# Attention scores, transposes and features in pairs of PSUM banks, emptied by one wide instruction each, and a new order of the work

## The chip, the cores and the metric

One core of a Trainium2 chip runs the whole kernel. The metric is the device time of one execution in microseconds (us). The engines are TensorE (PE; its weight loads are PEld), VectorE (DVE), ScalarE (ACT), GpSimd (POOL) and SyncE (SP, which here only issues DMAs).

## What is computed

Attention over 4 batches and 8 heads (768 positions, head size 64) with a mask from hashed buckets, followed by a gated MLP:

```
q_bucket, k_bucket = sign bits of q @ proj, k @ proj (6 bits)
scores = where(q_bucket == k_bucket, q @ k.T / 8, -1e9)
attn   = softmax(scores) (sum + 1e-9);  o = attn @ v;  x = heads of o side by side
h = gelu(x @ w_in);  u, v = halves of h;  v_n = layernorm(v) * g_ln
out = x + (u * (w_sg @ v_n + b_sg)) @ w_out
```

## The kernel before, in words

**Stages.** The attention works on 16 pairs of heads. For a pair, `parts` transposes q and k on PE (L475), and splits each into a high part (ACT, L479) and a low part (DVE, L482). `features` turns them into bucket features (PE L497, DVE L500). `largest` makes, for each of 6 tiles of 128 queries, scores with the queries on the partitions (PE L517) and takes the negative maximum of each row (DVE L524). `shift` joins the maxima of three tiles (DVE L532, L533), spreads them over columns (PE L539) and writes them into a row of the query features (ACT L545). `weigh` makes the scores again with the keys on the partitions (PE L560), now shifted by that row; ACT takes their exponentials (L566), and POOL adds these up (L576). `weighted` multiplies them with v (PE L589); `finish` sums over partitions (PE L604), copies sums and products out (ACT L607, L609), sends the sums through DRAM, adds 1e-9 (DVE L614), inverts (L615), and scales (DVE L625, POOL L626). A half pair is 384 queries: three tiles of `largest`, six key tiles of `weigh`, one `weighted`, one `finish`.

Beside this DVE splits the MLP's input weights into high and low parts, in 16 jobs of eight DVE instructions (`weight_job`, L356 to L365, with a square on POOL, L358). Then the MLP runs batch by batch: `hidden_v` (PE L761), `hidden_u` (L793), `gate` (L811), `project` (L837, L842), each with its evacuations. `gate_weights` transposes `w_sg` once (PE L720, ACT L726, DVE L729), and `out_weights` runs 16 smaller weight jobs, after the attention's buffers are given back.

**PSUM.** There are 8 banks of 128x512 floats. Every PE group takes single banks (`ps_tile`). The two heads of a pair run side by side on the two halves of PE's rows, so a group of `largest` takes two banks (four matmuls, two a bank) and a group of `weigh` two (eight matmuls). Each bank is emptied by an instruction of its own.

**The order.** All work is added to a planner (`Plan`) in groups with a cost, a priority and dependencies; its list scheduler picks for each engine the ready group of smallest priority and writes one fixed order per engine, in which the engine then issues. Priorities come from numbers at the top of the file (L22 to L30): `AHEAD` says how many tiles `largest` runs ahead of `weigh`, `WSTEP` and `WP` when the weight jobs are due, `wg` and `wo` when gate and output weights are. An instruction whose operand isn't ready holds up what stands behind it on its engine.

```
plan.add(PE, 0.346, prio + 0.01 * kh, lambda kh=kh: mm(kh), [...], sc[kh], form="row")
for j in range(2):
    plan.add(DVE, 0.55, prio, lambda j=j, kh=kh: nc.vector.tensor_reduce(
        mx()[:, kh, i, j:j + 1], sc[kh][j]()[:, :SH], axis=AX.X, op=ALU.max, negate=True), ...)
```

Of the kernel before, what the change touches and what calls it, by code (L numbers as in the profile page):

```python
# [29 lines left out]
ADDS = ["POOL", "POOL", "POOL", "POOL", "POOL"]  # L30


class Plan:
# [68 lines left out]
    def order(self):  # L102
# [32 lines left out]
        while len(out) < len(G):  # L135
# [59 lines left out]
            for b in wants[n]:  # L195
                b.i = min(b.slots, key=b.slots.get)
                b.slots[b.i] = 1e9
            for b in g["slots"]:
                left[b] -= 1
                till[b] = max(till.get(b, 0), end)  # L200
                if not left[b]:
                    b.slots[b.i] = till[b] + self.WAIT
# [20 lines left out]
def kernel(  # L223
# [54 lines left out]
    nc.vector.memset(less, -1.0)  # L278

# [137 lines left out]
    if True:  # L417
# [18 lines left out]
        NPT = 17  # L436
        ptiles = [late.pool.tile([P, SH + 1], F32, tag=f"p{i}", name=f"p{i}", bufs=1) for i in range(NPT)]
        for i, t in enumerate(ptiles):
            (nc.vector if i % 2 else nc.gpsimd).memset(t[:, SH:SH + 1], 1.0)
# [26 lines left out]
        def parts(st, s, prio):  # L466

            hh, lo, raw, fac = st.hi[s], st.lo[s], st.raw[s], (SCALE, 1.0)[s]
            for hf in range(2):
                tp = ps_tile()  # L470
                cs = slice(hf * SH, (hf + 1) * SH)

                def tr(tp=tp, hf=hf):
                    for i in range(HT):
                        nc.tensor.transpose(tp()[:, i * P:(i + 1) * P],  # L475
                                            raw()[:, hf * HT + i].rearrange("p j d -> p (j d)"), ident)

                def high(tp=tp, cs=cs):
                    nc.scalar.mul(hh()[:, cs], tp()[:, :SH], fac)  # L479

                def low(tp=tp, cs=cs):
                    nc.vector.scalar_tensor_tensor(lo()[:, cs], tp()[:, :SH], fac, hh()[:, cs].bitcast(F32),  # L482
                                                   op0=ALU.mult, op1=ALU.subtract)

                plan.add(PE, 0.327, prio, tr, [raw, (hh, hf), (lo, hf)], [tp])
                plan.add(ACT, 0.49, prio, high, [tp], [(hh, hf)])
                plan.add(DVE, 0.55, prio, low, [tp, (hh, hf)], [(lo, hf)])

        def features(st, s, prio):
            hh, lo, ft = st.hi[s], st.lo[s], st.ft[s]  # L490
            for hf in range(2):
                cs = slice(hf * SH, (hf + 1) * SH)
                fp = ps_tile()

                def project(fp=fp, cs=cs):
                    for i, (w, x) in enumerate(((pwh, hh), (pwl, hh), (pwh, lo))):
                        nc.tensor.matmul(fp()[:, :SH], w[:, s, :], x()[:, cs], start=(i == 0), stop=(i == 2))  # L497

                def sign(fp=fp, cs=cs):
                    nc.vector.tensor_scalar(ft()[:, cs], fp()[:, :SH], fcol[:, 2 * s:2 * s + 1],  # L500
                                            fcol[:, 2 * s + 1:2 * s + 2], op0=ALU.is_gt, op1=ALU.mult)

                plan.add(PE, 0.522, prio, project, [(hh, hf), (lo, hf), (ft, hf)], [fp])
                plan.add(DVE, 0.67, prio, sign, [fp], [(ft, hf)])

        def largest(st, t, prio):
# [5 lines left out]
            sc = [[ps_tile() for j in range(2)] for kh in range(2)]  # L512

            def mm(kh):
                for n, x in enumerate((st.ft, st.hi)):
                    for j in range(2):
                        nc.tensor.matmul(sc[kh][j]()[:, :SH], x[0]()[row(j), qs], x[1]()[row(j), kh * SH:(kh + 1) * SH],  # L517
                                         start=(n == 0), stop=(n == 1))

            for kh in range(2):  # L520
                plan.add(PE, 0.346, prio + 0.01 * kh, lambda kh=kh: mm(kh),
                         [(st.hi[0], hf), (st.hi[1], kh), (st.ft[0], hf), (st.ft[1], kh)], sc[kh], form="row")
                for j in range(2):
# [381 lines left out]
```

## Time and profile before

| | |
|---|---|
| median of 3 runs | 813.07 us (812.31 to 813.81) |
| the profiled execution | 810.48 us |
| its span, first to last instruction | 808.6 us |
| PE busy | 777.6 us, 96% |
| DVE busy | 594.6 us, 74% |
| POOL busy | 446.9 us, 55% |
| ACT busy | 410.9 us, 51% |
| mean granted TensorE clock | 0.976 of full speed |

The profiled execution lies 2.6 us below the median of the runs, and its span 1.9 us below its own time. A busy time counts an instruction from its start to its end, waits inside it included. PE's busy share says little here: a matmul that waits behind another counts as busy. The granted clock is 1 at 2.4 GHz and 0.5 at 1.2 GHz.

### The profile page before, as it was taken

To read this page: it belongs to the slowest core of one execution; us is meant where nothing else is said; L and a number is where in the kernel's file an instruction comes from. 1 tells how busy PE (TensorE), PEld (TensorE's weight loads), DVE (VectorE), ACT (ScalarE), POOL (GpSimd) and SP (SyncE) were. 2 spreads that over 40 slices of the span, in tenths; PEclk is the share of its full clock that TensorE was granted. 3 is DMA by queue.
4 is the path that set the end of the run, shared out by engine and by line. 5 is a ranking of instruction groups with operands and counts; after the bars stand their busy time and mean duration, and the time that the engine had idled before them with its cause. 6 is when DMAs were issued, how large, how long until landed. Compare 5 with 4: busy or idle time off the path is not lost.

```text
span 808.6 us, 15333 instructions
## 1 busy us (share of the span) xinstructions
PE 777.6 (96%) x5480; PEld 627.0 (78%) x5480; DVE 594.6 (74%) x1241; ACT 410.9 (51%) x926; POOL 446.9 (55%) x471
## 2 busy tenths in 40 slices
PE   6999999999899999999999999699899999999998
PEld 4877776767676767777676769598898889988996
DVE  7889988797988988988998449878981268407730
ACT  2457666665465656756575655614442246214411
POOL 1459787888688868888887962332232202501130
PEclk9799999999799999999999999699999999999999
DMA  6131432243243133243311112510034220040003
GB/s 156 40 82 38 130 99 73 82 112 89 64 112 96 51 93 89 58 99 93 88 46 54 29 41 62 198 51 27 26 92 157 84 73 21 19 131 27 1 1 130
DMA packets 99307, 60.93 MB, mean 75 GB/s; under 512 B 64288, under 2 KB 91040, under 8 KB 99232
## 3 DMA queue, kind: packets, MB, share of 16 engines
q1 hardware_dynamic: 97920, 56.94, 25.6%
q10 hardware_dynamic: 1312, 3.02, 1.1%
q8 instruction: 43, 0.70, 0.4%
q14 instruction: 32, 0.26, 0.1%
HBM read 47.16 MB, written 12.78 MB: 74 GB/s over the span
## 4 chain that ended last, share of the span: by engine, by line
PE 79%; DVE 17%; DMA 1%; issue 1%; ACT 1%; ACTq 0%; SPq 0%; DVEq 0%
PE g L560 16%; PE g L589 13%; PE g L811 12%; PE g L837 8%; PE g L517 7%; PE g L761 6%; PE g L793 5%; PE g L497 4%; DVE mx L524 3%; PE g L475 3%; PE g L604 2%; PE g L539 1%; PE g L842 1%; DVE h L746 1%; DVE wx L363 1%
## 5 line engine op out<-in xcount | busy, mean ns | idle before, releaser
L576 POOL TENSOR_TENSOR sum<-sum,p 128x384 f32<-128x384 f32 x256 | 257.4, 1041 | 41.0 <-ACT p L566 40.8
L524 DVE TENSOR_REDUCE mx<-g 128x1 f32<-128x384 f32 x384 | 186.9, 549 | 27.6 <-PE g L517 22.7
L566 ACT ACTIVATE p<-g 128x384 f32<-128x384 f32 x384 | 161.4, 495 | 53.5 <-PE g L560 49.5
L589 PE MATMUL g<-p,v 128*64 128x385 f32 x768 | 131.2, 491 | 0.0
L589 PEld LDWEIGHTS g<-p,v 128*64 128x64 f32 x768 | 52.3, 137 | 64.5 <-issue 61.4
L560 PE MATMUL g<-hq,hk 64*128 64x384 f32 x384 | 81.6, 372 | 8.3 <-DVE mx L524 8.1
L517 PE MATMUL g<-fk,fq 64*128 64x384 f32 x384 | 76.4, 350 | 1.7 <-DVE mx L524 0.8
L822 POOL TENSOR_TENSOR gs<-gt,gs 128x384 fp32r<-128x384 f32 x32 | 32.9, 1031 | 76.2 <-ACT gs L819 76.2
L576 POOL TENSOR_TENSOR sum<-p,p 128x384 f32<-128x384 f32 x64 | 67.0, 1065 | 14.3 <-ACT p L566 14.3
L560 PE MATMUL g<-hq,lk 64*128 64x384 f32 x384 | 74.6, 343 | 0.0
L517 PE MATMUL g<-hk,hq 64*128 64x384 f32 x384 | 73.8, 342 | 0.0
L560 PE MATMUL g<-fq,fk 64*128 64x384 f32 x384 | 73.5, 340 | 0.0
L560 PE MATMUL g<-lq,hk 64*128 64x384 f32 x384 | 73.4, 340 | 0.0
L771 POOL TENSOR_TENSOR mv<-mv,epsr 128x1 f32<-128x1 f32 x24 | 13.5, 562 | 108.0 <-DVE mv L770 101.7
L746 DVE SCALAR_TENSOR_TENSOR h<-h,g 128x384 f32<-128x384 f32 (+1 forms) x56 | 32.6, 605 | 55.0 <-ACT h L745 55.0
L837 PE MATMUL g<-woh,gs 128*128 128x512 f32 x192 | 65.4, 401 | 0.0
L811 PE MATMUL g<-wgh,zl 128*128 128x384 f32 x192 | 64.3, 335 | 0.0
L811 PE MATMUL g<-wgh,zh 128*128 128x384 f32 x192 | 64.3, 335 | 0.0
L811 PE MATMUL g<-wgl,zh 128*128 128x384 f32 x192 | 64.2, 334 | 0.0
L560 PEld LDWEIGHTS g<-hq,hk 64*128 64x128 f32 x384 | 44.4, 189 | 23.7 <-DVE mx L524 11.7
L814 DVE TENSOR_TENSOR gt<-g,b_bc 128x384 f32<-128x384 f32 x32 | 17.8, 555 | 52.8 <-PE g L811 32.4
L609 ACT COPY un<-g 128x385 f32<-128x385 f32 x32 | 15.4, 480 | 79.2 <-PE g L589 75.6
(126 smaller groups left out, 1779.8 us busy)
## 6 DMA issues: line engine op xcount, KB each, us to landing
q<-in_q_dram SPq DMA_DIRECT2D x32, 192.0 KB
k<-in_k_dram SPq DMA_DIRECT2D x32, 192.0 KB
v<-in_v_dram SPq DMA_DIRECT2D x16, 384.0 KB
rs<-r SPq DMA_DIRECT2D x64, 96.0 KB
xs<-xt SPq DMA_DIRECT2D x32, 192.0 KB
x<-xs SPq DMA_DIRECT2D x16, 384.0 KB
rx<-xs SPq DMA_DIRECT2D x96, 64.0 KB
out_dram<-ob SPq DMA_DIRECT2D x24, 256.0 KB
```

The lines of the kernel that those rows point to most:

```text
L517: nc.tensor.matmul(sc[kh][j]()[:, :SH], x[0]()[row(j), qs], x[1]()[row(j), kh * SH:(kh + 1) * SH], start=(n == 0), stop=(n == 1))
L524: plan.add(DVE, 0.55, prio, lambda j=j, kh=kh: nc.vector.tensor_reduce(mx()[:, kh, i, j:j + 1], sc[kh][j]()[:, :SH], axis=AX.X, op=ALU.max ...
L560: nc.tensor.matmul(sc[i][j]()[:, :SH], x()[row(j), ks], y()[row(j), cs], start=(n == 0), stop=(n == 3))
L566: plan.add(ACT, 0.495, prio, lambda i=i, j=j: nc.scalar.activation(p[i][j]()[:, :SH], sc[i][j]()[:, :SH], AF.Exp), [sc[i][j]], [p[i][j]])
L576: (nc.gpsimd if e == POOL else nc.vector).tensor_add(sums[j](), first()[:, :SH], p[i][j]()[:, :SH])
L589: nc.tensor.matmul(av()[row(j), :SH + 1], st.v()[:, j, kt, :], p[kt][j](), start=(kt == 0), stop=(kt == NT - 1))
L746: plan.add(DVE, us + 0.07, prio, lambda: nc.vector.scalar_tensor_tensor(h2()[:, :n], h2()[:, :n], 1.0 / GA, ps()[:, :n], op0=ALU.add, op1= ...
L761: nc.tensor.matmul(ps(), x()[:, ts_], w[:, c, FH:FF], start=(c == 0 and n == 0), stop=(c == NC - 1 and n == 2))
L793: nc.tensor.matmul(ps()[:, :SH], w[:, c, fs], x()[:, cs], start=(c == 0 and n == 0), stop=(c == NC - 1 and n == 2))
L811: nc.tensor.matmul(vp()[:, :SH], z()[:, t, fs], w()[:, t, cs], start=(t == 0 and n == 0), stop=(t == NT - 1 and n == 2))
L822: nc.gpsimd if e == POOL else nc.vector).tensor_sub(gl()[:, cs], gt(), gh()[:, cs].bitcast(F32)),
L837: nc.tensor.matmul(po(), a()[:, ts_], w()[:, f, :], start=(f == 0 and n == 0), stop=False)
```

## The change

One PSUM tile `psb` of 8 banks takes the place of eight. The planner's `slot` has a width: two-bank slots are the aligned pairs (0,1), (2,3), (4,5), (6,7), a pair being free when both banks are; a single bank goes by preference where its neighbour is in use. `largest`, `weigh`, `parts` and `features` take pairs, and one instruction over both banks (128x2x384) does what two did: the maximum, the exponential, the high and low part, the sign. `parts` and `features` now handle a whole tensor (six transposes, six matmuls) in one group. `spread`, `weighted`, `total` and the MLP take single banks. The exponentials lie in 8 tiles of two halves instead of 17 single ones, the sums in one tile of two halves; POOL's additions stay two per key tile (`ADDW` is 1). In `shift` one instruction takes the minimum of both halves and of `EMPTY` (L532 is gone); 1e-9 is added by ACT's copy of the sums (L614 is gone). The numbers that set the order change: the first weight job is due first of all and the others are further apart, `AHEAD` is 4, and the output weights' priority is nearer the front.

```
-MLP = {"xl": "POOL", "gm": "DVE", "gl": "POOL", "wg": 398.29, "wo": 46.93, "x": 568.79}
-HID = 198.49
-AVP = 3.75
-S0P = 0.02
-AHEAD = 5
-PREP, SHIFTP, FINP, WSTEP, WP = 0.96, 0.15, 1.7, 12, 7.76
+MLP = {"xl": "POOL", "gm": "DVE", "gl": "POOL", "wg": 434.12, "wo": 12.91, "x": 469.98}
+HID = 260.1
+AVP = 2.39
+S0P = 1.18
+AHEAD = 4
+PREP, SHIFTP, FINP, WSTEP, WP = 5.65, -1.32, 4.0, 37.92, -61.79
...
+    def place(self, b, t=1e9):
+        s = b.slots
+        if b.width == 2:
+            return min((max(s[i], s[i + 1]), i) for i in range(0, len(s), 2))
+        return min((max(s[i], t), -s[i ^ 1], -s[i], i) for i in s)[0::3]
...
+    psb = ps_s.pool.tile([P, 8, 512], F32, name="psb", tag="psb", bufs=1)
...
-        NPT = 17
+        NPT = 8
...
+            plan.add(PE, 0.654, prio, tr, [raw, hh, lo], [tp])
+            plan.add(ACT, 0.81, prio, high, [tp], [hh])
+            plan.add(DVE, 0.95, prio, low, [tp, hh], [lo])
...
+            plan.add(PE, 1.044, prio, project, [hh, lo, ft], [fp])
+            plan.add(DVE, 1.07, prio, sign, [fp], [ft])
...
-            sc = [[ps_tile() for j in range(2)] for kh in range(2)]
+            sc = [ps_two() for kh in range(2)]
...
-                for j in range(2):
-                    plan.add(DVE, 0.55, prio, lambda j=j, kh=kh: nc.vector.tensor_reduce(
-                        mx()[:, kh, i, j:j + 1], sc[kh][j]()[:, :SH], axis=AX.X, op=ALU.max, negate=True),
-                        [sc[kh][j]], [(mx, (kh, j, i))])
+                plan.add(DVE, 0.95, prio, lambda kh=kh: nc.vector.tensor_reduce(
+                    mx()[:, kh, i, :], sc[kh]()[:, :, :SH], axis=AX.X, op=ALU.max, negate=True), [sc[kh]], [(mx, (kh, i))])
...
-            plan.add(DVE, 0.16, prio, lambda: V.tensor_tensor(mx()[:, 0], mx()[:, 0], mx()[:, 1], op=ALU.min), [mx], [mx], port=True)
             plan.add(DVE, 0.16, prio, lambda: V.scalar_tensor_tensor(
-                m()[:, :, MROW::BL], mx()[:, 0], EMPTY, mx()[:, 0], op0=ALU.is_lt, op1=ALU.mult),
+                m()[:, :, MROW::BL], mx()[:, 0], EMPTY, mx()[:, 1], op0=ALU.min, op1=ALU.min),
...
-                    plan.add(ACT, 0.495, prio, lambda i=i, j=j: nc.scalar.activation(p[i][j]()[:, :SH], sc[i][j]()[:, :SH], AF.Exp),
-                             [sc[i][j]], [p[i][j]])
+                plan.add(ACT, 0.81, prio, lambda i=i: nc.scalar.activation(p[i]()[:, :, :SH], sc[i]()[:, :, :SH], AF.Exp),
+                         [sc[i]], [p[i]])
...
-            plan.add(ACT, 0.32, prio, lambda: nc.scalar.copy(sm(), tp()[:, :QH2]), [tp], [sm])
+            plan.add(ACT, 0.32, prio, lambda: nc.scalar.activation(sm(), tp()[:, :QH2], AF.Identity, bias=tiny[:, 0:1]), [tp], [sm])
...
-            plan.add(DVE, 0.16, prio, lambda: V.tensor_single_scalar(sq(), sq(), 1e-9, op=ALU.add), [sq], [sq], port=True)
```

In the rows below the lines of the kernel after are L474 for L456 (load of q and k), L349 for L338 (load of weights), L367 to L376 for L356 to L365 (weight job), L498 for L482, L514 for L500, L531 for L517, L536 for L524, L543 for L533, L549 for L539, L569 for L560, L597 for L589, L612 for L604, L724 for L720, L765 for L761, L797 for L793.

In the names, q, k, v are loaded tensors, hq, lq, hk, lk high and low parts, fq, fk features, w, wx, wy, wg the buffers of a weight job, p exponentials, sum their sums, gs the raw `w_sg`; g and psb are PSUM.

**The start, SP and DVE.** SP's first rows before:

```order
L456 DMA q_258<-in_q_dram 128x6x64 x2
L456 DMA k_261<-in_k_dram 128x6x64 x2
L462 DMA v_264<-in_v_dram 128x2x384
L462 DMA v_266<-in_v_dram 128x2x384
L338 DMA w_0_268<-in_moe_w_in_dram 128x512
```

and now:

```order
L349 DMA w_0_242<-in_moe_w_in_dram 128x512
L474 DMA q_244<-in_q_dram 128x6x64 x2
L474 DMA k_247<-in_k_dram 128x6x64 x2
L480 DMA v_250<-in_v_dram 128x2x384
L480 DMA v_252<-in_v_dram 128x2x384
L349 DMA w_1_270<-in_moe_w_in_dram 128x512
```

DVE up to the first signs, now (before, its first low part L482 stood where L370 stands here, with no weight job ahead of it, and the first weight job lay between the signs):

```order
L370 SCALAR_TENSOR_TENSOR wx_256<-wg_258,wx_256 128x256
L372 TENSOR_SCALAR wy_254<-wx_256 128x256
L373 SCALAR_TENSOR_TENSOR wy_254<-w_0_242,wy_254 128x256
L374 TENSOR_TENSOR wx_256<-wx_256,wy_254 128x256
L376 SCALAR_TENSOR_TENSOR wil<-wx_256,wih 128x256
L498 SCALAR_TENSOR_TENSOR lq_0_285<-psb,hq_0_274 128x768
L498 SCALAR_TENSOR_TENSOR lk_0_298<-psb,hk_0_293 128x768
L367 TENSOR_SCALAR wy_302<-w_1_270 128x256
...
L374 TENSOR_TENSOR wx_310<-wx_310,wy_302 128x256
L514 TENSOR_SCALAR fq_0_318<-psb,fcol 128x768
```

The first weight job moved ahead of the first low part, and the second ahead of the first sign; on SP the load of `w_0` moved ahead of q and k.

**PE around a half pair's shift.** `m` is the row of maxima that L539 (now L549) spreads. Before, at pair 2:

```order
L517 MATMUL g_1116_2390<-hk_2_2197,hq_2_2188 128x384
L589 MATMUL g_1116_2395<-p_161,v_1779 64x385
...
L589 MATMUL g_1116_2395<-p_155,v_1779 64x385
L604 MATMUL g_1116_2426<-sum_2240,ones 32x192 x2
L604 MATMUL g_1116_2426<-sum_2260,ones 32x192 x2
L539 MATMUL g_1116_2435<-identr,m_105 128x128 x3
L560 MATMUL g_1116_2443<-hq_2_1751,hk_2_1760 128x384
```

and now, at pair 4:

```order
L531 MATMUL psb<-hk_4_2713,hq_4_2686 128x384 x2
L569 MATMUL psb<-hq_4_2686,hk_4_2713 128x384 x2
...
L569 MATMUL psb<-fq_4_2853,fk_4_2877 128x384 x2
L511 MATMUL psb<-hq_4_3016,pwh 128x384
...
L511 MATMUL psb<-lq_4_3041,pwh 128x384
L549 MATMUL psb<-identr,m_108 128x128 x3
L511 MATMUL psb<-hk_4_3053,pwh 128x384
...
L597 MATMUL psb<-p_152,v_2733 64x385 x2
```

Between a half's last maxima matmuls and the spread stood the 12 long matmuls of `weighted`; now sixteen of `weigh` and six of `features` stand there (in the other half six or twelve transposes), and `weighted` follows the spread.

**PE at the gate weights.** Before, the 36 transposes of `w_sg` ran in one block between `hidden_u` and nine matmuls of the next `hidden_v`; now twelve of these stand ahead and six inside:

```order
L797 MATMUL psb<-xh_2136,wil 128x384
L765 MATMUL psb<-wih,xh_5909 128x512
...
L765 MATMUL psb<-wih,xl_5923 128x512
L724 MATMUL psb<-ident,gs_5937 128x128 x6
L724 MATMUL psb<-ident,gs_5947 128x128 x3
L765 MATMUL psb<-wih,xh_5973 128x512
...
L765 MATMUL psb<-wih,xl_5999 128x512
L724 MATMUL psb<-ident,gs_5947 128x128 x3
L724 MATMUL psb<-ident,gs_5952 128x128 x6
```

The first transposes moved behind twelve other matmuls, and 27 of the 36 still stand together after that.

## Rows read from the trace of the kernel before

**Rows 1.** The page of the profile, parts 1 and 4: the span, the busy time of the engines (busy us, share of the span, instructions), and the shares of the chain of waits by engine.
```profile
span 808.6 us, 15333 instructions
PE 777.6 (96%) x5480; PEld 627.0 (78%) x5480; DVE 594.6 (74%) x1241; ACT 410.9 (51%) x926; POOL 446.9 (55%) x471
PE 79%; DVE 17%; DMA 1%; issue 1%; ACT 1%; ACTq 0%; SPq 0%; DVEq 0%
```

**Rows 2.** The busy time of each engine by stretches of the span (us from its start). The columns are the stretch, its length, then PE, PEld, DVE, ACT and POOL busy us with their instructions in brackets, the granted TensorE clock as a share of the full one, the DMA share and GB/s.
```profile
0.00:25.20 25.20, 17.56 (x84) 13.59 (x86) 19.25 (x72) 5.08 (x9) 2.23 (x17) 0.88 0.48 125
25.20:210.00 184.80, 182.14 (x1556) 134.61 (x1554) 160.20 (x318) 115.10 (x278) 148.41 (x148) 0.99 0.33 85
210.00:225.00 15.00, 11.69 (x82) 10.03 (x80) 13.55 (x21) 8.28 (x20) 9.39 (x9) 0.66 0.21 67
225.00:480.00 255.00, 250.71 (x2126) 181.04 (x2123) 210.12 (x414) 159.10 (x388) 210.13 (x214) 1.00 0.28 72
505.00:525.00 20.00, 13.63 (x58) 11.52 (x57) 16.65 (x35) 12.32 (x28) 7.79 (x6) 0.66 0.59 196
578.00:586.00 8.00, 4.96 (x20) 4.64 (x19) 7.76 (x23) 4.81 (x9) 2.47 (x3) 0.79 0.12 33
```

**Rows 3.** The chain of waits in order of time, pieces in the attention stage: start us, length us, what. They are the undisturbed passes of each kind of matmul group, and the pass over one pair's values at two times.
```profile
46.51 1.39 PE g L560 x16
47.90 0.69 PE g L517 x8
50.68 1.46 PE g L475 x12
52.14 4.03 PE g L589 x24
56.17 0.46 PE g L604 x8
56.63 0.48 PE g L539 x3
57.11 2.17 PE g L497 x12
59.28 1.59 PE g L560 x16
...
424.30 4.03 PE g L589 x24
```

**Rows 4.** The groups of instructions by line, shapes kept apart: line, engine, operation, out<-in, shapes, count | busy us, mean ns of one | idle time before them and who ended it.
```profile
L524 DVE TENSOR_REDUCE mx<-g 128x1 f32<-128x384 f32 x384 | 186.9, 549 | 27.6 <-PE g L517 22.7
L532 DVE TENSOR_TENSOR mx<-mx 128x6 f32<-128x6 f32 x32 | 16.1, 504 | 0.4
L533 DVE SCALAR_TENSOR_TENSOR m<-mx 128x6 fp32r<-128x6 f32 x32 | 21.8, 680 | 1.0
L614 DVE TENSOR_SCALAR sq<-sq 128x6 f32<-128x6 f32 x32 | 11.3, 352 | 0.1
L750 DVE SCALAR_TENSOR_TENSOR u<-h,g 128x384 f32<-128x384 f32 x32 | 16.5, 548 | 4.4 <-ACT h L748 3.9
L750 DVE SCALAR_TENSOR_TENSOR y<-h,g 128x512 f32<-128x512 f32 x24 | 16.3, 681 | 3.5 <-ACT h L748 3.4
L623 ACT ACTIVATE e<-rs,less 128x384 f32<-128x384 f32 x32 | 19.9, 621 | 0.0
```

**Rows 5.** The timeline of DVE, SP and PE in the first 30 us: start us, length us, engine, line, operation, out<-in, shapes, count, and in brackets the idle time before and who ended it.
```profile
0.73 1.55 SPq L456 DMA_DIRECT2D q<-in_q_dram  x2
7.34 0.47 SPq L338 DMA_DIRECT2D w<-in_moe_w_in_dram  x1
7.47 1.51 PE L475 MATMUL g<-ident,q 128*128 128x128 f32 x6 [4.08 <-DMA q<-in_q_dram]
25.16 0.52 PE L560 MATMUL g<-hq,hk 64*128 64x384 f32 x2
11.93 0.37 DVE L356 TENSOR_SCALAR wy<-w 128x256 int32<-128x256 int32 x1
15.37 5.66 DVE L524 TENSOR_REDUCE mx<-g 128x1 f32<-128x384 f32 x12
```

**Rows 6.** The timeline of all engines between 203 and 216 us, the same columns.
```profile
208.92 0.55 PE L539 MATMUL g<-identr,m 128*128 128x128 f32 x3
209.13 2.24 POOL L576 TENSOR_TENSOR sum<-sum,p 128x384 f32<-128x384 f32 x2
211.33 1.85 POOL L694 TENSOR_TENSOR xl<-x,xh 128x768 fp32r<-128x768 f32 x1
211.56 1.91 DVE L362 SCALAR_TENSOR_TENSOR wy<-w,wy 128x256 f32<-128x256 uint32 x1
214.44 1.15 PE L560 MATMUL g<-hq,hk 64*128 64x384 f32 x2 [3.31 <-DVE mx L524]
```

**Rows 7.** Who waited for whom between 25 and 480 us, PE's weight loads (PEld, which stand ahead of each matmul): us in total, times, longest us.
```profile
PEld g L560 <- DVE mx L524: 11.7, 12, 3.6
PEld g L539 <- DVE m L533: 3.5, 7, 0.7
```

**Rows 8.** The same between 480 and 600 us.
```profile
PEld g L720 <- DVE wgl L729: 4.8, 2, 3.7
PEld g L793 <- DVE y L750: 3.4, 1, 3.4
```

More of the change, by code (lines that the diff above doesn't have):

```diff
@@ L125, in when @@
         def when(n):
-            return max([at[n]] + [sorted(b.slots.values())[i] for i, b in enumerate(wants[n])])
+            return max([at[n]] + [min(b.slots.values()) if b.width == 1 else self.place(b)[0] for b in wants[n]])
         for g in G:
@@ L195, in order @@
             for b in wants[n]:
-                b.i = min(b.slots, key=b.slots.get)
-                b.slots[b.i] = 1e9
+                b.i = self.place(b, start)[1]
+                for i in range(b.i, b.i + b.width):
+                    b.slots[i] = 1e9
             for b in g["slots"]:
@@ L201, in order @@
                 if not left[b]:
-                    b.slots[b.i] = till[b] + self.WAIT
+                    for i in range(b.i, b.i + b.width):
+                        b.slots[i] = till[b] + self.WAIT
             for m in users[n]:
@@ L433 @@
             pass
-        NPT = 17
-        ptiles = [late.pool.tile([P, SH + 1], F32, tag=f"p{i}", name=f"p{i}", bufs=1) for i in range(NPT)]
+        NPT = 8
+        ptiles = [late.pool.tile([P, 2, SH + 1], F32, tag=f"p{i}", name=f"p{i}", bufs=1) for i in range(NPT)]
         for i, t in enumerate(ptiles):
-            (nc.vector if i % 2 else nc.gpsimd).memset(t[:, SH:SH + 1], 1.0)
+            (nc.vector if i % 2 else nc.gpsimd).memset(t[:, :, SH:SH + 1], 1.0)
         def p_tile():
@@ L446, in row, with two @@
             return slice(j * D, (j + 1) * D)
+        def two(t):
+            return t().rearrange("p (a b) -> p a b", a=2)
         def load(n, prio):
@@ L486, in parts, with high @@
-                plan.add(ACT, 0.49, prio, high, [tp], [(hh, hf)])
-                plan.add(DVE, 0.55, prio, low, [tp, (hh, hf)], [(lo, hf)])
-        def features(st, s, prio):
[L490 to L495, printed above, removed]
-                    for i, (w, x) in enumerate(((pwh, hh), (pwl, hh), (pwh, lo))):
[L497 to L504, printed above, removed]
+            def high():
+                nc.scalar.mul(two(hh), tp()[:, :, :SH], fac)
@@ L588, in product @@
                     for j in range(2):
-                        nc.tensor.matmul(av()[row(j), :SH + 1], st.v()[:, j, kt, :], p[kt][j](), start=(kt == 0), stop=(kt == NT - 1))
-            plan.add(PE, 1.3 * HT, prio, product, [t for two in p for t in two] + [st.v], [av], form="col")
+                        nc.tensor.matmul(av()[row(j), :SH + 1], st.v()[:, j, kt, :], p[kt]()[:, j, :], start=(kt == 0), stop=(kt == NT - 1))
+            plan.add(PE, 1.3 * HT, prio, product, p + [st.v], [av], form="col")
         def finish(st, hf, prio):
-            av, sums, tp = st.av, st.sum, ps_tile()
+            av, sums, tp = st.av, st.sum, ps_one()
             sm, e = late.ring([P, QH2], F32, "sm", 3), late.ring([P, SH], F32, "e", 3)
```

106 lines of the change are left out of this document (54 added, 52 removed).

## The prediction

> **What bounds the kernel now.** I read the page first. PE is busy for 96% of the span, and the chain of waits runs over PE for 79% and over DVE for 17% [rows 1]. The change takes no matmul away, so it can only return time in which PE stands or runs slowly; the 17% on DVE says where to look. The table of stretches comes next: from 25.2 to 480 us, the attention, DVE is busy for 160.2 + 13.6 + 210.1 = 383.9 of 454.8 us, or 84%, and POOL for 367.9 us [rows 2].
>
> How much PE loses in the attention has to be counted, since a waiting matmul counts as busy. The chain shows undisturbed passes [rows 3]: a `weigh` of two key tiles 1.39 us, a maxima tile 0.69, twelve transposes 1.46, `weighted` 4.03, `total` 0.46, a spread 0.48, twelve feature matmuls 2.17. A pair of heads needs 6 x 1.39 + 6 x 0.69 + 1.46 + 2 x 4.03 + 2 x 0.46 + 2 x 0.48 + 2.17 = 26.05 us. A `weigh` behind another kind of matmul takes 1.59, so three such turns add 0.6: 26.65 us. The two `weighted` passes in the rows, at 52.14 and 424.30, lie 13 pairs apart: 28.63 us a pair. **PE loses 2.0 us a pair, some 32 us over 16 pairs.** That is the first purse.
>
> Where it goes: PE's weight loads wait for maxima (L524) for 11.7 us and spreads wait for their row (L533) for 3.5 us [rows 7]. The longest such wait shows how. POOL and DVE's weight job meet: L362 takes 1.91 us from 211.56 on, while POOL runs a subtraction of 1.85 us from 211.33 on, where another step of such a job took 0.37 with POOL idle [rows 5, 6]; the maxima stand behind it on DVE, and PE's `weigh` starts at 214.44 after 3.31 us [rows 6]. In that stretch the granted clock is 0.66 [rows 2], so 15 x (1 - 0.66) / 0.5 = 10.2 us ran at 1.2 GHz instead of 2.4, which costs up to 5.1 us. The rest of the 32, some 12 us, is small waits and hand-overs that no row gathers.
>
> The second purse lies behind the attention. From 505 to 525 us PE waits for the gate weights' evacuation (4.8 us) at a clock of 0.66, around 578 us for a gelu (3.4 us) at 0.79 [rows 2, 8]. The half clock there costs up to 6.8 + 1.7 us, of which the waits hide a part; together about 13 us.
>
> **DVE gets lighter.** A reduction of 384 columns starts every 5.66 / 12 = 0.472 us when nothing else is in the way [rows 5]. From 384 to 512 columns the same line's duration grows from 548 to 681 ns, 1.04 ns a column [rows 4]. 384 columns more thus cost 0.399 us, and a wide instruction returns 0.073 us against two narrow ones. A pair has 12 wide maxima, 2 low parts and 2 signs: 16 x 0.073 = 1.17 us. L532 goes, 2 x 0.504; L614 goes, 2 x 0.352 [rows 4]. That makes 2.9 us a pair of about 24.2 (84% of 28.63). ACT's additive copy in place of L614 and its halved number of exponentials lie beside PE, and I cost them at nothing; their cover is ACT's idle half [rows 1].
>
> The Trainium skill (Perfetto Trace Analysis, Optimizing Scalar/DVE Operations) puts the overhead of a DVE instruction on PSUM at about 125 ns and advises grouping on a saturated engine. An estimate by that page would be 16 x 0.125 + 1.7 = 3.7 us a pair instead of 2.9; the pitch in these rows is smaller, and I stay with it.
>
> **What PE gains of it.** The relief is slack, not time: it shortens only waits that DVE ends last. Those are (11.7 + 3.5) / 16 = 0.95 us a pair, plus 5.1 / 16 = 0.3 of half clock, plus a part of the small waits. The slow weight-job steps stay, as POOL's additions do, and meet the same maxima; so I let the named waits halve (-0.5), most of the half clock go (-0.2) and little of the rest (-0.1). 16 x -0.8 = **-13 us**. The bounds: nothing, if the weight job's steps alone set the waits, and three quarters of the purse, -24.
>
> **The start.** SP now issues `w_0` ahead of q. Before, q was issued at 0.73 and PE could start at 7.47 [rows 5]; a weight load takes SP 0.47 us [rows 5], and its bytes move ahead of q's. Issue and landing took 6.7 us before; I take 1.2 us of delay, between that issue of 0.5 and 2. On DVE the first weight job fits into the wait for q, but the second stands around the signs, and a third's three steps ahead of the maxima: ten steps of about 0.4 us [rows 5] and a low part of the next pair, where five stood between the signs before; about +3. The first wide low part waits for six transposes instead of three. Against this only four maxima tiles and not six stand ahead of the first `weigh`, which starts at 25.16 now [rows 5], and PE transposes and projects the next pair meanwhile (1.46 + 2.17 us of work done early, less 2 x 0.69 put off). I expect the first `weigh` some 3 us later with 2 us more done: **+1.5 us**, between -3 and +4.
>
> **Behind the attention.** The gate weights come 2.8 us later relative to `hidden_u`, with the output weights' jobs spread forward; 27 transposes in a block still wait for DVE. I take **-3 us** of the 13, between +2 and -8.
>
> The number of PE's changes between kinds of matmul stays as good as the same, and the MLP's banks are single as before: nothing.
>
> **Sum.** -13 + 1.5 - 3 = -14.5 us on the profiled execution's 810.5, or 796; that execution lies 2.6 us below the median of the runs, so I forecast **798 us** as the median, 791 to 805 for this case alone.
>
> **The rivals.**
>
> *A, deeper.* DVE's slack lets every maximum arrive in time, and PE no longer falls to the half clock. For it: with no weight job in the way, passes of 1.39 and 0.69 us follow each other without a gap [rows 3]. Against: the slow steps of rows 6 stay. -24 + 1.5 - 7 = -29.5: 783 us.
>
> *B, the spread becomes late.* Before, `weighted`'s 4.03 us lay between the last maxima matmuls and the spread. Now it is a `weigh` and six feature matmuls or transposes, 1.39 + 0.7 to 1.1 us. The second of two wide maxima ends about 0.2 + 2 x 0.87 us behind the last matmul, and L533's successor adds 0.68 [rows 4], in all 2.6 against 2.1 to 2.5. If 0.3 us is lost 32 times, 9.6 us go: 808 us.
>
> *C, slower, for lack of banks.* In PSUM eight single banks become four pairs, and a lone single bank spoils one. A maxima tile holds two pairs, a `weigh` two; with four there is no spare. Each half pair, ACT runs two `e` steps of 0.62 us (L623 and its follower) [rows 4] among the exponentials; a pair then comes back up to 1.24 us late, and `weigh` and the maxima behind it wait. If 0.8 of it reaches PE in each of 32 halves, that is 25.6 us: 824 us. It decides from 0.47 us a half on. Against: before, the same steps held back four banks of eight, and the waits that rows 7 names are on DVE; DVE's pairs also come back in one step, earlier than the second of two banks did.
>
> The Trainium skill speaks for C in two places of the page Perfetto Trace Analysis: matmul groups should rotate through different PSUM banks (Matmuls), and where DVE or ACT are not saturated but cause bubbles elsewhere, breaking instructions up may help (Optimizing Scalar/DVE Operations), the opposite of this change. DVE at 84% lies between the two cases.
>
> *D, the wide instruction saves nothing:* it costs two narrow ones. Then DVE is lighter by 1.7 us a pair only, and -13 shrinks to -7.5: 804 us.
>
> **How the numbers follow.** A measurement here can tell about 0.2%, 1.6 us, from no change. Forecast 0.46, A 0.20, B 0.14, C 0.14, D 0.06. C is slower. Of B's spread of some 5 us about a third lies within 811.5 to 814.7, of D's a sixth. Faster 0.46 + 0.20 + 0.09 + 0.05 = 0.80; same 0.05 + 0.01 = 0.06; slower 0.14. The range leaves out C and the end of A: 780 to 814.
>
> **What would show it.** Right: wide reductions of about 0.95 us at a pitch of 0.87; DVE below 80% busy between 30 and 470 us; `weighted` passes 27.8 us apart per pair; waits for maxima halved; a first `weigh` near 28 us. Wrong: spreads that wait for L543 (B); PE's weight loads waiting for exponentials or maxima in most half pairs, with pairs 28.6 us apart or more (C); a reduction of 1.1 us (D); pairs below 27.3 us (A). A `weigh` that starts by 25 us would refute my term for the start.

## The result, and the profile after

The changed kernel takes 814.89 us (median of 20 runs, 811.98 to 822.28) against 811.38 us before (20 runs, 809.80 to 813.81); the ratio is 1.0052, 95% interval 1.0031 to 1.0073. It is slower by half a per cent, where 798 us and a gain were forecast. The profiled execution of it took 815.91 us, span 814.1 us.

The page, its span, busy times and chain of waits, as [rows 1]:

```profile
span 814.1 us, 14589 instructions
PE 772.9 (95%) x5480; PEld 614.5 (75%) x5480; DVE 553.7 (68%) x918; ACT 403.5 (50%) x702; POOL 427.9 (53%) x466
PE 80%; DVE 14%; DMA 2%; issue 2%; ACT 1%; POOL 0%; SPq 0%; ACTq 0%; DVEq 0%
```

DVE lost 41 us of busy time, and PE gained nothing. The groups by line, shapes apart, as [rows 4], and two stretches as [rows 2] (the length, then PE, PEld, DVE, ACT, POOL busy us, granted clock, DMA share, GB/s):

```profile
L536 DVE TENSOR_REDUCE mx<-psb 128x2 f32<-128x768 f32 x192 | 174.1, 949 | 62.3 <-PE psb L531 59.0 <-ACT p L573 2.4 <-ACT h L749 0.6
L543 DVE SCALAR_TENSOR_TENSOR m<-mx 128x6 fp32r<-128x6 f32 x32 | 18.0, 564 | 1.0
L573 ACT ACTIVATE p<-psb 128x768 f32<-128x768 f32 x192 | 146.5, 812 | 71.6 <-PE psb L569 68.5 <-DVE sq L622 1.9 <-POOL sum L586 0.6
```
```profile
25.20:480.00 454.80, 442.56 (x3771) 317.74 (x3771) 342.80 (x446) 275.99 (x462) 347.37 (x368) 0.99 0.29 75
39.00:56.00 17.00, 12.64 (x108) 9.15 (x106) 16.48 (x22) 9.58 (x17) 12.24 (x13) 0.91 0.10 32
```

A wide reduction takes 949 ns where two narrow ones took 2 x 549, as forecast; DVE is 75% busy in the attention instead of 84%. But in the 17 us from 39 on DVE is full and PE does 12.64 us. Who waited for whom, as [rows 7, 8]; the rows ahead of the dots from 25 to 480 us, the others from 480 to 600:

```profile
PEld psb L569 <- DVE mx L536: 7.2, 10, 2.9
PEld psb L531 <- ACT p L573: 6.5, 25, 0.4
PEld psb L511 <- DVE mx L536: 5.3, 5, 1.5
PEld psb L569 <- ACT p L573: 4.8, 16, 0.3
PEld psb L491 <- DVE mx L536: 3.2, 4, 2.0
PEld psb L549 <- DVE m L543: 0.5, 2, 0.3
...
PEld psb L724 <- DVE u L754: 8.9, 4, 4.1
PEld psb L815 <- DVE u L754: 3.3, 1, 3.3
```

**Where the time went.** To compare kernels that order their work differently I give every matmul the pitch it has undisturbed (the median distance to the next of its kind; 0.087 us in `largest` and `weigh`, from [rows 3]: 1.39 / 16) and add these up in the order of execution, 732 us for each kernel. The table shows how long a kernel's profiled execution took for the first 80 us of this matmul work (the start), from there to 440 (the attention) and from there to the end of the span. All kernels of the experiments stand in it.

| kernel | median, us | to 80 | 80 to 440 | 440 to end |
|---|---|---|---|---|
| before | 811.4 | 104.2 | 411.5 | 292.9 |
| changed | 814.9 | 115.1 | 400.3 | 298.7 |
| e1_jobs | 821.1 | 108.0 | 412.8 | 297.5 |
| e2_mlp | 818.4 | 113.9 | 408.2 | 297.8 |
| e3_both | 819.8 | 110.0 | 413.6 | 296.5 |
| e4_allnum | 801.8 | 110.6 | 394.5 | 292.1 |
| e5_attnum | 801.9 | 109.4 | 394.6 | 295.9 |
| e5b_hid_mlp | 806.4 | 112.2 | 394.2 | 297.9 |
| e6_hid | 820.1 | 115.1 | 405.0 | 298.6 |
| e7_sp_loads | 818.7 | 115.6 | 404.8 | 297.4 |
| e8_no_adds | 798.8 | 105.4 | 392.9 | 298.2 |
| e11_before_no_adds | 797.5 | 103.0 | 400.0 | 292.8 |
| e12_allnum_no_adds | 795.9 | 109.7 | 392.3 | 292.1 |
| e13_best | 804.9 | 109.0 | 394.1 | 300.9 |
| e14_row_on_act | 811.4 | 112.4 | 399.3 | 298.1 |

The attention gains 11.2 us, the start loses 10.9, the stage behind the attention 5.8: +5.5 us between the two profiled executions, +3.5 between the medians. Executions of one order differ too: e4 and e5b run the same instructions in the same order for 500 us, and stand 1.6 us apart at 80 us of work.

### The profile page after: what moved, and what is told of

Same layout as the page of the kernel before. It is cut to its first block, busy times and chain, and to the rows that moved or that the text cites. A ratio compares the mean times of both kernels' runs of the same rounds, so it can differ in the third digit from the quotient of the medians.

```text
span 814.1 us, 14589 instructions
## 1 busy us (share of the span) xinstructions
PE 772.9 (95%) x5480; PEld 614.5 (75%) x5480; DVE 553.7 (68%) x918; ACT 403.5 (50%) x702; POOL 427.9 (53%) x466
## 4 chain that ended last, share of the span: by engine, by line
PE 80%; DVE 14%; DMA 2%; issue 2%; ACT 1%; POOL 0%; SPq 0%; ACTq 0%; DVEq 0%
PE psb L597 15%; PE psb L569 14%; PE psb L815 10%; PE psb L841 8%; PE psb L531 8%; PE psb L765 7%; PE psb L797 6%; PE psb L511 4%; DVE mx L536 4%; PE psb L491 3%; PE psb L612 1%; PE psb L846 1%; PE psb L549 1%; DVE wy L367 1%; DVE owx L368 1%
## 5 line engine op out<-in xcount | busy, mean ns | idle before, releaser
L536 DVE TENSOR_REDUCE mx<-psb 128x2 f32<-128x768 f32 x192 | 174.1, 949 | 62.3 <-PE psb L531 59.0
L573 ACT ACTIVATE p<-psb 128x768 f32<-128x768 f32 x192 | 146.5, 812 | 71.6 <-PE psb L569 68.5
L597 PE MATMUL psb<-p,v 128*64 128x385 f32 x768 | 133.5, 498 | 0.0
L597 PEld LDWEIGHTS psb<-p,v 128*64 128x64 f32 x768 | 52.9, 138 | 64.8 <-issue 62.0
L531 PE MATMUL psb<-fk,fq 64*128 64x384 f32 x384 | 72.8, 374 | 4.5 <-DVE mx L536 1.7
L569 PE MATMUL psb<-hq,hk 64*128 64x384 f32 x384 | 69.6, 356 | 5.3 <-DVE mx L536 4.6
L815 PE MATMUL psb<-wgh,zh 128*128 128x384 f32 x192 | 65.3, 340 | 4.4 <-DVE u L754 3.0
L841 PE MATMUL psb<-woh,gs 128*128 128x512 f32 x192 | 65.5, 402 | 0.0
L531 PE MATMUL psb<-hk,hq 64*128 64x384 f32 x384 | 65.3, 335 | 0.0
L569 PE MATMUL psb<-fq,fk 64*128 64x384 f32 x384 | 65.3, 334 | 0.0
L569 PE MATMUL psb<-hq,lk 64*128 64x384 f32 x384 | 65.2, 333 | 0.0
L569 PE MATMUL psb<-lq,hk 64*128 64x384 f32 x384 | 65.2, 333 | 0.0
L531 PEld LDWEIGHTS psb<-fk,fq 64*128 64x128 f32 x384 | 36.1, 184 | 32.0 <-issue 15.8
```

The source lines that it names most:

```text
L531: nc.tensor.matmul(sc[kh]()[:, j, :SH], x[0]()[row(j), qs], x[1]()[row(j), kh * SH:(kh + 1) * SH], start=(n == 0), stop=(n == 1))
L536: plan.add(DVE, 0.95, prio, lambda kh=kh: nc.vector.tensor_reduce(mx()[:, kh, i, :], sc[kh]()[:, :, :SH], axis=AX.X, op=ALU.max, negate=Tr ...
L569: nc.tensor.matmul(sc[i]()[:, j, :SH], x()[row(j), ks], y()[row(j), cs], start=(n == 0), stop=(n == 3))
L573: plan.add(ACT, 0.81, prio, lambda i=i: nc.scalar.activation(p[i]()[:, :, :SH], sc[i]()[:, :, :SH], AF.Exp), [sc[i]], [p[i]])
L597: nc.tensor.matmul(av()[row(j), :SH + 1], st.v()[:, j, kt, :], p[kt]()[:, j, :], start=(kt == 0), stop=(kt == NT - 1))
L815: nc.tensor.matmul(vp()[:, :SH], z()[:, t, fs], w()[:, t, cs], start=(t == 0 and n == 0), stop=(t == NT - 1 and n == 2))
```

## The experiments

Each has 4 to 12 runs, beside 11 to 17 of the kernel before on the same chip. The first four put back numbers of the order.

**e1_jobs, e2_mlp, e3_both, e4_allnum.** The edits, all in the changed kernel:

```
e1:   WSTEP, WP = 37.92, -61.79                       ->  12, 7.76
e2:   "wg": 434.12, "wo": 12.91, "x": 469.98          ->  398.29, 46.93, 568.79
e3:   e1 and e2
e4:   e3 and HID, AVP, S0P, AHEAD, PREP, SHIFTP, FINP ->  198.49, 3.75, 0.02, 5, 0.96, 0.15, 1.7
```

> The changed kernel with the due times of the input weights' jobs as before (WSTEP 12, WP 7.76 in place of 37.92, -61.79); all else as changed. Theory 'numbers': PE lost some 11 us against the kernel before by its 80th us of matmul work (115.2 against 104.3 us of time) because the first weight jobs stand ahead of the signs and maxima on DVE, and its loads ahead of q on SP. With the old due times w_0 is behind q again, that loss falls to 3 us or less and most of it stays: 804 to 808 us. Rival 'conserved': a job's steps cost PE the same wherever they stand; the start gets better by 5 us or more, but the loss comes back between 120 and 250 us as in the kernel before (stall at 211 us): 813 to 816. Rival 'banks': four pairs are too few while the pipe fills, whatever the jobs do: the 80th us of work stays at 112 us or later, 814 to 816.

> The changed kernel with the MLP's due times as before (wg 398.29, wo 46.93, x 568.79 in place of 434.12, 12.91, 469.98); HID and the attention as changed. Theory 'numbers': the output weights' jobs now stand on DVE ahead of the gelus of hidden_u and of the gate weights' low parts, and PE, level with the kernel before at 440 us of work (515.7 and 515.9), loses 4.9 us up to 480 us of work. With the old due times the wait of the gate weights' transposes for DVE u falls from 8.9 us to 5 or less, the gate's first matmul comes at 528 us or earlier instead of 532.1, total 809.5 to 811.5. Rival 'banks': single banks are now handed out by another rule and the wait is for a bank that no due time frees: 532 us, 814 to 816. Rival 'x': what is late is the second batch's x, loaded later still with 568.79: 816 or more.

> The changed kernel with both edits: the input weights' jobs due as before and the MLP's due times as before. If both losses are due to these numbers and independent, the gains of the two runs add up: by 'numbers' 800 to 804 us. If the first is conserved and only the second counts, 809 to 811. If both are due to the banks, 814 to 816.

> The changed kernel with every number of the order as before (HID 198.49, AVP 3.75, S0P 0.02, AHEAD 5, PREP 0.96, SHIFTP 0.15, FINP 1.7, WSTEP 12, WP 7.76, and the MLP's): the pairs of banks, the wide instructions and the two removed DVE operations alone. 'Numbers': the prediction's attention term holds when the start and the MLP are as before: first weigh at 25 to 27 us, pairs of heads some 27.9 us apart, gate at 513 to 518 us, total 798 to 803. 'Banks': with five maxima tiles ahead on four pairs the weigh waits for pairs; pairs of heads 28.5 us apart or more, total 810 to 824.

Measured: e1 821.1 us, ratio 1.0123 (1.0099 to 1.0146); e2 818.4, 1.0090 (1.0057 to 1.0123); e3 819.8, 1.0113 (1.0094 to 1.0133); e4 801.8, **0.9881** (0.9861 to 0.9902). My theory 'numbers' missed in e1 to e3: the start gets 7.1 us better in e1 and the attention gives it all back ('conserved', but dearer than it said), and the MLP's three numbers are worth next to nothing behind the attention. It hit in e4's total: with all numbers of before, pairs, wide instructions and the two removed operations gain 1.2%, the attention 17 us. Only the first `weigh` comes late there, at 31.6 us. Pairs of heads lie 27.6 us apart there: the chain of waits has two `weighted` passes 11 pairs apart, (401.61 - 98.29) / 11.

```profile
98.29 4.03 PE psb L597 x24
...
401.61 4.03 PE psb L597 x24
```

So the cause had to be sought in the attention's numbers or HID, and in something that a table of single waits had not told. e2's trace told it. DVE, POOL and PE of e2 at 206 us:

```profile
206.41 5.58 DVE L543 SCALAR_TENSOR_TENSOR m<-mx 128x6 fp32r<-128x6 f32 x1
205.63 6.33 POOL L586 TENSOR_TENSOR sum<-sum,p 128x384 f32<-128x384 f32 x7
212.04 0.90 PE L549 MATMUL psb<-identr,m 128*128 128x128 f32 x3 [4.53 <-DVE m L543]
```

L543 joins the maxima: six columns. It takes 5.58 us and ends with POOL's seventh addition; the spread behind it starts after 4.53 us of waiting, and behind this idle time PE goes on at half the clock (the stretch that follows, columns as above: granted 0.50):

```profile
212.00:218.50 6.50, 6.46 (x21) 3.89 (x23) 2.39 (x3) 0.94 (x2) 0.00 (x0) 0.50 0.08 17
```

In the shown execution of the changed kernel the same two instructions stand so:

```profile
207.78 0.26 DVE L543 SCALAR_TENSOR_TENSOR m<-mx 128x6 fp32r<-128x6 f32 x1
207.01 6.37 POOL L586 TENSOR_TENSOR sum<-sum,p 128x384 f32<-128x384 f32 x7
```

The order of the two kernels is the same up to 515 us; the times of this one step are 5.3 us apart, and the attention takes 408.2 us in e2 and 400.3 here. That could be how runs of one kernel come to 812 and to 821 us. It is not the only way there: the profiled executions of e1 and e3, at 820 and 822 us, have no L543 above 1.06 us. New theory: DVE's small steps that work in SBUF (the memory on the chip that holds all tiles but those in PSUM) wait for POOL's additions.

**e5_attnum, e5b_hid_mlp, e7_sp_loads, e8_no_adds.**

```
e5:   HID, WSTEP, WP, MLP as changed; AVP, S0P, AHEAD, PREP, SHIFTP, FINP as before
e5b:  HID, MLP as changed; all else as before
e7:   - eng.dma_start(w(), sg_v[t])              + nc.sync.dma_start(w(), sg_v[t])
e8:   - lambda ...: nc.gpsimd.tensor_add(...)    + lambda ...: first and nc.gpsimd.tensor_add(...)
```

> The changed kernel with the attention's numbers alone as before (AHEAD 5, S0P 0.02, AVP 3.75, PREP 0.96, SHIFTP 0.15, FINP 1.7); the input weights' jobs (WSTEP 37.92, WP -61.79), HID 260.1 and the MLP's numbers as changed. Theory 'lead': one maxima tile less ahead and the moved spread are what PE pays for from the 80th us of work on and at the end of the attention; from 100 to 400 us of work it needs 326 to 329 us as in the run with all numbers of before (326.5), not 331.7 as changed; the start stays late through the weight jobs (80 us of work at 112 us or later), total 804 to 809. Rival 'jobs': the loss follows the weight jobs' due times; 331 us or more in that stretch, 812 to 818.

> The changed kernel with the attention's and the jobs' numbers as before and only HID 260.1 and the MLP's numbers (wg 434.12, wo 12.91, x 469.98) as changed. Beside the run with every number of before it has these four numbers alone. Theory 'MLP numbers': the loss between 440 and 480 us of matmul work (47.0 us of time as changed, 40.6 with all numbers of before) is theirs: 45 to 47 us there, total 806 to 808. Rival 'order': it comes from how the attention hands over, and these numbers do nothing: 41 us, 800 to 803.

> The changed kernel, its order kept, with the six loads of the gate weights issued by SP and not by ACT. In the changed kernel ACT stands still from 506.9 to 514.0 us, its third such load and the tanh of a gelu behind it, until a load of x has landed; the gate weights' transposes then wait for that gelu's end on DVE (8.9 us). Theory 'ACT's queue': without loads in ACT's queue the tanh runs at once, the wait for DVE u falls to 4 us or less, the gate's first matmul comes 3 to 6 us earlier (526 to 529 us), total 809 to 812. Rival 'transfers': what is late are the loads themselves, the transposes then wait for the weights, 532 us or later, total 814 to 818.

> The changed kernel, its order kept, with 256 of POOL's 320 additions left out: only the first of each five is made, so the denominators hold two key tiles of six. POOL is then nearly idle in the attention. Theory 'port': steps of DVE that work in SBUF wait while POOL adds (the spread's row L543 takes 0.56 us on average for 6 columns, the jobs' steps up to 0.9 us more than their shortest); without the additions L543 falls to 0.2 us, DVE's excess of 48 us between 30 and 470 us falls below 10, and from 100 to 400 us of work PE needs 326 to 328 us instead of 331.7; the two long gaps at 44 and 53 us shrink by a half; total 803 to 808. Rival 'lead': PE's gaps are for maxima in PSUM, whose reductions do not slow beside POOL: 330 us or more, 812 to 816.

e5: 801.9 us, 0.9877 (0.9865 to 0.9890), better than 'lead' had it, at the start too (109.4 us, not 112 or later); the attention's six numbers together are worth 13 us (one by one they weren't tried). They move L543: its mean falls from 564 to 282 ns, and 6 of 32 take over 0.4 us where 22 did. e4 has the same:

```profile
L543 DVE SCALAR_TENSOR_TENSOR m<-mx 128x6 fp32r<-128x6 f32 x32 | 8.4, 262 | 0.5
```

e5b: 806.4, 0.9929 (0.9915 to 0.9944), in the total as 'MLP numbers' said: HID and the MLP's numbers cost 4.6 us on top of e4, but only 2.4 of it between 440 and 480 us of work (43.0 us there, not 45 to 47).

e7: 818.7, 1.0068 (1.0045 to 1.0092); the profiled execution has L543's long wait (5.58 us at 208.20), so the total says little here. From the last `weighted` matmul to the gate's first it is 52.7 us instead of 55.0: the transposes' wait for `u` falls from 8.9 to 4.1 us, but one of 2.7 us for a step of the output weights' jobs (L368) comes in. ACT's blocked queue, which this shows in the changed kernel, is worth about 2 us, not 3 to 6:

```profile
505.93 0.93 ACTq L716 DMA_DIRECT2D gs<-in_moe_w_sg_dram  x2
506.50 0.89 ACT L749 ACTIVATE h<-psb 128x384 f32<-128x384 f32 x2
513.13 0.85 ACTq L716 DMA_DIRECT2D gs<-in_moe_w_sg_dram  x2
514.02 0.52 ACT L752 ACTIVATE h<-h 128x384 f32<-128x384 f32 x1 [6.63 <-DMA x<-xs]
```

e8: **798.8 us, 0.9840** (0.9827 to 0.9852). With the order untouched and 256 of POOL's 320 additions left out, 16 us go, more than 'port' had it: 9.7 at the start, 7.4 in the attention. L543 takes 173 ns, none above 0.29 us:

```profile
L543 DVE SCALAR_TENSOR_TENSOR m<-mx 128x6 fp32r<-128x6 f32 x32 | 5.5, 173 | 1.0
```

The start shows the rest. DVE and POOL of the changed kernel from 48.6 us on, a weight job between maxima, and PE's wait behind it:

```profile
48.60 1.05 DVE L370 SCALAR_TENSOR_TENSOR wx<-wg,wx 128x256 f32<-128x256 f32 x1
49.69 1.00 DVE L372 TENSOR_SCALAR wy<-wx 128x256 int32<-128x256 int32 x1
50.73 0.97 DVE L373 SCALAR_TENSOR_TENSOR wy<-w,wy 128x256 f32<-128x256 uint32 x1
51.73 1.10 DVE L374 TENSOR_TENSOR wx<-wx,wy 128x256 f32<-128x256 f32 x1
52.75 1.81 DVE L536 TENSOR_REDUCE mx<-psb 128x2 f32<-128x768 f32 x2
49.33 8.02 POOL L586 TENSOR_TENSOR sum<-sum,p 128x384 f32<-128x384 f32 x8
53.75 0.69 PE L569 MATMUL psb<-hq,hk 64*128 64x384 f32 x2 [2.61 <-DVE mx L536]
```

And the same steps of the same job in e8:

```profile
46.70 0.42 DVE L370 SCALAR_TENSOR_TENSOR wx<-wg,wx 128x256 f32<-128x256 f32 x1
47.16 0.29 DVE L372 TENSOR_SCALAR wy<-wx 128x256 int32<-128x256 int32 x1
47.49 0.43 DVE L373 SCALAR_TENSOR_TENSOR wy<-w,wy 128x256 f32<-128x256 uint32 x1
47.95 0.42 DVE L374 TENSOR_TENSOR wx<-wx,wy 128x256 f32<-128x256 f32 x1
48.29 1.81 DVE L536 TENSOR_REDUCE mx<-psb 128x2 f32<-128x768 f32 x2
```

Four steps take 4.12 us beside additions and 1.56 without; the reductions behind them take 1.81 both times. In the changed kernel each of the four steps ends 0.16 to 0.28 us after an addition ends, one step to an addition.

**e11_before_no_adds, e12_allnum_no_adds, e13_best, e6_hid.**

```
e11:  kernel before;  + if kt > 1: return        (ahead of the addition)
e12:  e4 with e8's edit
e13:  e4 with WSTEP, WP = 37.92, -61.79
e6:   changed kernel with HID = 198.49
```

> The kernel before, its order kept, with 256 of POOL's 320 additions left out (the denominators hold two key tiles of six). Theory 'port': what the change gains in the attention with the numbers of before (14.4 us from 20 to 400 us of matmul work) is mostly that DVE's small steps meet POOL less often: L532 and L533 together lost 25.4 us in the kernel before, and 67 us of DVE's time in all went so. Without additions the kernel before then gains by itself: from 100 to 400 us of work 326 to 330 us instead of 342.2, total 792 to 798. Rival 'width': the gain is that of wide instructions on pairs of banks; then the kernel before without additions keeps most of its waits for maxima, 336 us or more there, total 802 to 808.

> The changed kernel with every number of the order as before, its order kept, and the same 256 additions left out. Theory 'port': it comes out within 4 us of the kernel before without additions, 790 to 796, since with POOL quiet neither has much to lose in the attention. 'Width': it is 8 us or more below the kernel before without additions. Theory 'lead': five maxima tiles ahead serve better than four whatever POOL does; it is then 5 us or more below the changed kernel without additions (798.8), and in the attention (100 to 400 us of work, 324.4 there) below 321.

> The changed kernel with every number as before except the input weights' jobs (WSTEP 37.92, WP -61.79 as changed). With those the first weighted pass came at 39.2 us instead of 43.3 and 20 us of work at 40.5 instead of 43.3; the old HID and MLP numbers were worth some 2 us from 400 us of work on. If the two parts add, 799 to 801 us; if the weight jobs meet other steps again, 801 to 804.

> The changed kernel with HID alone as before (198.49 instead of 260.1: hidden_v of the first batch, and so x, earlier; the gate weights then stand behind nine and not twelve matmuls of the second batch). Theory 'HID': the loss between 440 and 480 us of work (47.0 us instead of 42.3) is that of this number: 42 to 44 us there. Rival 'late queue': it is a matter of which load holds ACT's queue, and changes with every order: 46 us or more. The total is 809 to 816 by the first, 813 to 820 by the second; the spread's row keeps its delays by POOL, so runs several us apart are to be seen again.

e11: 797.5 us, 0.9824 (0.9808 to 0.9841); e12: 795.9, 0.9812 (0.9795 to 0.9828); both totals are as 'port' had them. This is the clearest result: **with POOL quiet the three kernels, 797.5, 795.9 and 798.8, lie within 3 us**; with POOL's additions they are 811.4, 801.8 and 814.9. POOL's additions cost 13.9, 5.9 and 16.1 us, and that makes most of the distances. By stages of the table they cost the kernel before 1.2 us at the start and 11.5 in the attention, the changed kernel 9.7 and 7.4, e4 0.9 and 2.2: the change eased the attention and brought the cost to the start. It need not all be DVE's: PE's `total` and ACT's exponentials also wait for the sums themselves, for 1.4 and 2.7 us before, 2.7 and 0.6 in the changed kernel, 1.3 and 3.1 in e4, and no run tells the two apart. 'Width' has its share in the attention: 400.0 against 392.3, so 7.7 of the 17 us that e4 gains there (the two removed operations among it) stay when POOL is quiet; at the start pairs lose 6.7 us (103.0, 109.7). 'Lead' falls: e12's attention is not better than e8's (392.3, 392.9). In e11 the additions that are left, one a head and half, still meet L532 and L533 (387 and 640 ns on average), so 13.9 is a lower bound. DVE and POOL of e11 at 81 us:

```profile
81.30 0.94 DVE L532 TENSOR_TENSOR mx<-mx 128x6 f32<-128x6 f32 x1
82.28 0.93 DVE L533 SCALAR_TENSOR_TENSOR m<-mx 128x6 fp32r<-128x6 f32 x1
81.22 1.00 POOL L628 TENSOR_TENSOR xt<-xt,e 128x384 f32<-128x384 f32 x1 [11.09 <-DVE sq L616]
82.18 1.98 POOL L578 TENSOR_TENSOR sum<-p,p 128x384 f32<-128x384 f32 x2
```

Each step ends with the POOL instruction beside it: 82.24 and 82.22, 83.21 and the first half of 82.18 to 84.16.

e13: 804.9, 0.9919 (0.9905 to 0.9933), above both of its forecasts: the parts don't add, the stage behind the attention loses 8.8 us against e4 though only the weight jobs' due times differ. e6: 820.1, 1.0107 (1.0089 to 1.0124): from 440 to 480 us of work still 45.2 us, between its two theories, and the whole stage takes 298.6 us as in the changed kernel, so HID is not what that stage lacks; the attention takes longer (405.0 us).

**e14_row_on_act.** The order of the changed kernel, all additions, L543 alone taken off DVE and given to ACT, as a copy times zero that leaves out the shift by the maximum.

```
- V.scalar_tensor_tensor(m()[:, :, MROW::BL], mx()[:, 0], EMPTY, mx()[:, 1], op0=ALU.min, op1=ALU.min)
+ nc.scalar.mul(m()[:, :, MROW::BL], mx()[:, 1], 0.0)
```

> The changed kernel, its order kept, with the spread's row made by ACT (a copy of the second half's maxima times zero, so the shift by the maximum is left out) in place of DVE's L543; POOL's additions all stay. Theory 'row': L543's waits for POOL are what the changed order pays for: 12.2 us of delays in the shown execution, and in others one wait of 5.4 us through seven additions at 206 us, which puts runs of one kernel at 812 and at 821. Without L543 on DVE no execution has that wait, the runs lie within 3 us of each other, from 100 to 400 us of work PE needs 327 to 329 us instead of 331.6, total 807 to 810. Rival 'jobs alone': what POOL costs is paid by the steps of the weight jobs, L543's delays are hidden behind other matmuls; 331 us or more in that stretch, runs up to 820 again, median 812 to 817.

811.4 us, 0.9993 (0.9979 to 1.0007), runs from 808.5 to 812.9. Between the two theories: the runs above 813 are gone and the median is 3.5 us lower, so L543 is worth about that and the long tail (less what 32 copies of 0.21 us cost ACT). By the busy times of its lines, beside those in e8, DVE loses about 26 us in the weight jobs' steps, 12.5 in L543 and 4.5 in `xt` (L632, 686 ns in the changed kernel, 548 in e8). I put the other 12.6 us down to e8 to the jobs' steps and `xt`, 7.0 of them at the start (112.4 and 105.4); no run changes these two alone.

## Why the prediction was wrong

**Held.** The costs of the instructions: 949 ns for a wide reduction, where about 0.95 us was forecast. The first `weigh`, forecast near 28 us, starts at 28.2. DVE is below 80% busy. The attention's term, -13 us between 0 and -24: -11.2 in the shown execution, 27.87 us a pair late in the attention, as this pair of rows shows (seven pairs), with 27.8 forecast:

```profile
225.26 4.03 PE psb L597 x24
...
420.33 4.03 PE psb L597 x24
```

The size is in part luck: in e2 and e7, which have the same order in the attention and L543's long wait, the gain is 3.3 and 6.7 us. Part of the gain in the shown execution is the half clock that I had named: from 210 to 225 us the granted clock is now 1.00, where it was 0.66 [rows 2]. And at least 11.5 us of the first purse were POOL's: without the additions the kernel before is that much shorter in the attention by itself. Of the 2.6 us that the sum adds for the median at its end, 0.9 are left with 20 runs of the kernel before.

**Rivals.** B: the spread waits 0.5 us in all for L543 where it waited 3.5 [rows 7]; but the traces of e2 and e7 have it at 4.53 us in one place, so B named a place where time can go, by another cause than the pass of `weighted`. C: weight loads do wait longer for exponentials, 6.5 and 4.8 us in all where it was 2.0 (L517) and 2.8 (L560), but never over 0.4 us, and pairs of heads lie closer, not further apart; the kernel is slower for another reason. D falls with 949 ns, A with pairs 27.87 us apart. One sign failed: the waits for maxima were to halve; L569's fall from 11.7 us [rows 7] to 7.2, but L511 and L491 now wait 5.3 and 3.2. Of the 7.2, 6.1 lie before 115 us, where the next paragraph looks.

**Failed: the start, +1.5 us (-3 to +4).** It is +10.9. I followed it up to the first `weigh`, where it held (28.2 us, and 1.7 us more matmul work done), and stopped there; the loss comes in the next 30 us, where PE waits 2.61 us at 53.75 behind a weight job. My count of ten job steps "of about 0.4 us" took the price from a place where POOL was idle. Beside additions a step takes 1 us (rows at 48.60 above). e8 gives back 9.7 of the 10.9. With POOL quiet in both kernels the changed start is 2.4 us longer (105.4 and 103.0), inside the range: what the term lacked was POOL. Either set of numbers put back also shortens it, the jobs' to 108.0 (e1), the attention's to 109.4 (e5), so it is how the two stand together. One part stays open: with every number as before the start on pairs of banks is 6.4 us longer (e4), and 6.7 with POOL quiet.

**Failed: behind the attention, -3 us (+2 to -8).** It is +5.8. The wait that I took to get a little shorter grew: the gate weights' transposes wait 8.9 us for `u` where they waited 4.8 for `wgl` [rows 8]. It is not POOL's, as it is 8.8 us in e8 too. ACT's queue stands behind a load for 6.63 us (2 us, e7); HID and the MLP's numbers cost e5b 4.6 us on top of e4. But e2 and e6 don't recover it and e13 loses it with those numbers back. The order there is one that a small shift spoils; what exactly, stays open.

**The step that I read wrongly.** I saw that POOL and a weight-job step met (1.91 us, [rows 6]), and that L532 and L533 take 504 and 680 ns for six columns [rows 4], and I put the first down as one slow step and the second as DVE's work that goes with the instruction. Both were the same wait: such a step takes 0.17 us when POOL is quiet (173 ns in e8), and 0.16 is the shortest of each line before, so of the two lines' time about 32 x (0.504 + 0.680 - 2 x 0.17) = 27 us were waits. What PE gains in e11 does not come from these two, though: 22 of the 27 us are still there, and 13.9 us are gone. By the lines' busy times DVE loses 20 us less in the weight jobs' steps there, and 9 less in L614 and `xt`. The forecast came close for the banks without the new numbers (801.8 us), but by other terms, +6.4, -17.0 and -0.8 us, so by luck. The new order brings L543 back beside the additions, and more of the jobs' steps (26 us of DVE's time against 14 in e4, by their lines' busy times with additions and without); L543 alone is worth 3.5 of the 13 us between the two (e14).

The Trainium skill (SBUF — State Buffer, Who interferes with whom) has the rule that I should have weighed: DVE and GpSimd share a port pair as an exclusive lock, held for a whole instruction, and a DVE instruction with two SBUF inputs contends with a GpSimd instruction that reads SBUF, a reduction does not. The traces agree: reductions take 949 ns with additions and 950 without, L543 564 and 173.

## What to carry to other kernels

A DVE instruction on a few columns that shows a mean of half a microsecond can be waiting, not working, as L532, L533 and L543 were: compare its shortest with its mean, look at what POOL runs at that moment, and see whether it ends when POOL's instruction ends. Cost a moved step at its price in the place it goes to. Numbers that set a static order are a change of their own: try the structure with the old ones first, as e4 does, and judge them against the neighbours that they bring together.

## What the runs showed of the hardware

Where L543 met POOL's additions, it mostly waited for the running one and took its turn before the next: 22 of 32 in the changed kernel take 0.4 to 1.05 us, none in e8 over 0.29. In two profiled executions (e2 at 206.41, e7 at 208.20) the same step got no turn for 5.58 us, until POOL's run of seven additions was over; in the shown execution, of the same order there, it took 0.26 us. The rule of the Trainium skill cited above (a lock for one instruction) does not foresee that; no run here shows what decides it. The changed kernel's runs differ by up to 10 us, and with L543 on another engine (e14) by 4.4; that this wait is the cause in each of the long runs is not shown, as one execution of them was profiled.
